# Attention with mirrored squares: consecutive key tiles, V in one transfer, and logits turned on VectorE

## The chip, the cores and the metric

The kernel runs on one core of a Trainium2 chip. A core has a matrix engine (TensorE, PE in the profile; PEld is its loading of weights), a vector engine (VectorE, DVE), a scalar engine (ScalarE, ACT), a general one (GpSimd, POOL), and a queue that issues transfers (SyncE, SP). Each of them takes its instructions in order; between them semaphores decide. Data lie in SBUF, 128 partitions wide, and matmul results in PSUM. The metric is the device time of one execution in microseconds.

## The reference

Eight batches of 2496 tokens go through an attention without softmax, and its output through a mixture of experts of which each token uses one.

```python
def _attn_ref(u, v, z):
    scale = 1.0 / S
    scores = scale * np.matmul(z, z.transpose(0, 2, 1))
    attn = np.maximum(scores, 0.0) ** 2
    out = np.matmul(attn, v)
    return u * out

def _moe_ref(x, w_gate, w1, w2):
    logits = x @ w_gate
    expert_idx = np.argmax(logits, axis=1)
    ...
    for e in range(E):
        xe = x[mask]
        h = np.maximum(xe @ w1[e], 0.0)
        out[mask] = gate_w[mask, None] * (h @ w2[e])
```

Here S is 2496, the width of `u` and `v` 256, that of `z` 64, and there are 8 experts with 1024 hidden values. Queries and keys are the same `z`, so the matrix of scores is symmetric: the square for query i and key j is that for query j and key i.

## The kernel before

**Numbers.** Matmuls take fp32r operands, which hold fewer bits than fp32. Each operand is therefore split into a rounded part and a remainder (`hi` and `lo` for the squares, two halves of `vt` for V), and products of the parts are summed. The sum over keys of one pair of key tiles is 12 matmuls (L319, L321, L322).

**Loops.** A batch has five chunks of queries, four of 512 and one of 448, and 20 key tiles of 128, taken in ten pairs `kp`. The last 64 rows of the last tile repeat tokens and count only with a remainder's part. A step is one (batch, chunk, pair); 400 steps are written out in one list, and step s computes the scores of step s + 2 (`LA = 2`) before its own weighted sums. The compiler's scheduler orders what the list leaves open. Work given to `pinned` stays behind what was last issued on each engine.

**Scores.** `scores` (L272) computes a pair's scores in PSUM, relu (L295) and square (L296) on ACT, `hi` on ACT or DVE (L298), `lo` on DVE (L300). By symmetry this is done only for pairs in key chunk `cc >= c`. Where `cc > c`, `turn` (L241) transposes the squares in blocks of 32 x 32 on DVE (L255), and writes 1 MB for four key tiles to DRAM (L258, `scr`). `bring` (L260) reads it back with partitions and blocks exchanged (L266), into a slot `s`, up to eight steps before it is used. For `cc < c`, `scores` then only splits what was brought (L285 on ACT, L286 on DVE).

**Key tiles.** A key tile isn't made of consecutive tokens. In the first four key chunks, tile i of a chunk holds tokens i, i + 4, i + 8 and so on (`rows_of`, L232); in the last, three tiles hold every third of 384 tokens and the fourth the 128 behind them. With this order, the turned squares lie in runs of 128 consecutive queries when they are read.

**V.** V must be in the order of the key tiles. `fetch_v` (L127) issues four transfers of 32 partitions for a pair in the first four key chunks, and six and four smaller ones for the two pairs of the last, all on SP, into two buffers `vr`. `split_v` (L143) makes the two parts: a cast on ACT (L146), a subtraction on POOL (L148). V of the next batch is fetched one pair a step during the last chunk of a batch, and split one step later, since it takes the place of the pair that was just used; in batch 0 it is fetched two steps ahead.

**From the sums to the experts.** Behind a chunk's ten steps `gate_x` (L336) multiplies by `u`, splits the result, and puts work into the list `bg`, of which one item is pinned to each step from the third of the next chunk on: `logits` (L365), `turn_rows` (L353), two empty items, `choose` (L407), `exps`, `place` (L428). `logits` multiplies by 16 columns of weights (8 experts, 2 parts), which leaves 16 partitions by n tokens in PSUM. ACT copies them (L374), DVE separates the 16-bit halves of each value (L379, L380), and two DMA transposes on SP (L382) put tokens on partitions. `choose` joins the halves (two copies, L411) and finds the expert; `place` computes each token's row in its expert's list, writes the rows (L453 on SP) and scatters token numbers (L458 on POOL). `turn_rows` transposes the rows themselves with four more DMA transposes (L363).

Behind all steps the experts run over tiles of tokens (`tiles`, `up` L735, `down` L756 and L758), with rows gathered on POOL and turned on SP (L703).

Of the kernel before, what the change touches and what calls it, by code (L numbers as in the profile page):

```python
# [23 lines left out]
E = 8  # L24
# [24 lines left out]
def fused_kernel(ctx: ExitStack, tc: tile.TileContext, zt, ut, v, wg, wcat, out):  # L49
# [77 lines left out]
    def fetch_v(b, kp):  # L127

        vr = vraw[b, kp] = sb.tile([P, 2, D], F32, name="vr", bufs=2)
        c, h = divmod(kp, 2)  # L130
        if c < NC_ - 1:
            for g in range(G):
                src = v[b, :, G * c + g, :].rearrange("(k i) d -> k i d", i=G)
                nc.sync.dma_start(vr[g * R:(g + 1) * R], src[:, 2 * h:2 * h + 2])
            return
        for i in range(2 * h, min(2 * h + 2, 3)):
            for k in range(3):
                lo, hi = -(-(k * P - i) // 3), min(P, -(-((k + 1) * P - i) // 3))
                nc.sync.dma_start(vr[lo:hi, i - 2 * h], v[b, bass.ds(3 * lo + i - k * P, hi - lo, step=3), G * c + k, :])  # L139
        if h:  # L140
            nc.sync.dma_start(vr[:, 1, :], v[b, :, NK - 1, :])
# [31 lines left out]
    wg2 = const.tile([P, 2, 2, E], FR, name="wg2")  # L173
# [33 lines left out]
    def constants():  # L207
        nc.vector.tensor_copy(wg2[:, :, 0, :], wg_sb)
        nc.vector.tensor_tensor(wg2[:, :, 1, :], wg_sb, wg2[:, :, 0, :].bitcast(F32), op=ALU.subtract)
# [31 lines left out]
    def turn(b, c, cc, h, a):  # L241
# [6 lines left out]
        t4_ = tt.rearrange("p (s r e) -> p s r e", s=G, r=4)  # L248
        for i in range(2):
            k = 2 * h + i  # L250
            if cc < NC_ - 1:
                to = t4_[:, :, :, k::4]
            else:
                to = t4_[:, :, :, k:3 * R:3] if k < 3 else t4_[:, :, :, 3 * R:]
            nc.vector.transpose(out=to, in_=a[:, i].rearrange("p (s q r) -> p s r q", s=G, r=4))  # L255
# [4 lines left out]
    def bring(b, cc, c):  # L260
# [7 lines left out]
        brought[b, cc, c] = st.rearrange("p (g r e) -> p r g e", g=G, r=4)  # L268
# [3 lines left out]
    def scores(b, c, kp):  # L272
# [63 lines left out]
    def gate_x(b, c, acc):  # L336
# [28 lines left out]
        def logits():  # L365
# [10 lines left out]
            if n < QC:  # L376
                nc.vector.memset(lp[:, :, n:QC], 0)
# [581 lines left out]
```

## Time and profile before

| | us |
|---|---|
| median of three runs | 2562.58 (2561.98 to 2563.81) |
| the profiled execution | 2576.18 |
| its span, first to last instruction | 2574.3 |
| PE busy | 2333.1 |
| DVE busy | 1754.4 |
| ACT busy | 1446.9 |
| POOL busy | 735.3 |
| mean granted TensorE clock | 0.948 |

The profile is of one execution, 0.5% above the median of the others. Lines such as L255 are those of the kernel listed above. Attention fills the first 1640 us or so, the experts the rest. A group of instructions is shown with its count, busy time in us, mean ns of one, and, behind the second bar, the idle time of its engine just before, with what ended it. A window gives for each engine its busy time and number of instructions. The granted clock is a share of full speed. SPq is the queue of SP, whose entries show how long it took to issue a transfer, not how long the transfer took.

### The profile page before, as it was taken

Reading aid. Unit: us, or ns where it says so; the run is one execution under the profiler, and the core shown is the slowest. Engines: PE = TensorE matmul, PEld = TensorE weight load, DVE = VectorE, ACT = ScalarE, POOL = GpSimd, SP = SyncE. Lnnn points to the kernel's source line nnn. Section 1 sums busy time; section 2 is a strip of 40 time slices with the busy share of each in tenths; the row PEclk is TensorE's granted clock in tenths of the full one; section 3 lists DMA queues with packets and bytes.
Section 4 is the critical chain, followed back from the end, with each engine's and each line's share of the span. In section 5 each row is a group of like instructions: output and inputs, shape, how many; then the busy total and the mean of one; then the engine's idle time right before and its main releaser. Section 6 shows DMA issues by size and latency. Waiting matters only on the chain.

```text
span 2574.3 us, 32216 instructions
## 1 busy us (share of the span) xinstructions
PE 2333.1 (91%) x10872; PEld 1947.0 (76%) x10872; DVE 1754.4 (68%) x3027; ACT 1446.9 (56%) x1993; POOL 735.3 (29%) x707
## 2 busy tenths in 40 slices
PE   7997987898889799789899798799999999999998
PEld 5785776687668677667678677688888888888887
DVE  6877866787777787766786786475556566556554
ACT  4755754664655575555565574345456456556554
POOL 2112113013112112112212221454445445445431
PEclk8998998999889899899899899899999999999999
DMA  5695896986878877688779589775456456547540
GB/s 161 172 185 118 216 160 105 194 176 124 191 153 152 193 165 149 177 162 153 166 170 171 129 198 201 134 177 143 129 148 171 144 153 174 150 151 188 143 138 26
DMA packets 329693, 406.00 MB, mean 158 GB/s; under 512 B 201708, under 2 KB 245498, under 8 KB 310064
## 3 DMA queue, kind: packets, MB, share of 16 engines
q1 hardware_dynamic: 298128, 284.77, 51.8%
q0 software_dynamic: 31392, 119.10, 15.9%
q8 instruction: 87, 1.43, 0.2%
q14 instruction: 86, 0.70, 0.1%
HBM read 233.67 MB, written 127.32 MB: 140 GB/s over the span
## 4 chain that ended last, share of the span: by engine, by line
PE 54%; DMA 17%; DVE 16%; issue 4%; SPq 4%; ACT 4%; POOL 1%; DVEq 0%; ACTq 0%; POOLq 0%
PE ph L735 16%; PE y L756 11%; DMA vr<-in_v_dram 7%; DMA lg<-lp 7%; PE acc L322 6%; PE acc L321 6%; PE y L758 6%; PE acc L319 6%; DVE s L255 5%; DVE tlo L300 3%; SPq L139 2%; DVE tlo L286 2%; PE ps_s L293 2%; PE ps_s L294 1%; ACT tf L295 1%
## 5 line engine op out<-in xcount | busy, mean ns | idle before, releaser
L321 PE MATMUL acc<-tlo,t 128*128 128x512 f32 (+1 forms) x1520 | 616.5, 406 | 85.0 <-DVE tlo L300 53.9
L319 PE MATMUL acc<-thi,t 128*128 128x512 f32 (+1 forms) x1600 | 603.5, 402 | 54.5 <-ACT thi L285 26.5
L322 PE MATMUL acc<-thi,t 128*128 128x512 f32 (+1 forms) x1600 | 638.3, 400 | 3.7 <-POOL t L148 3.2
L321 PEld LDWEIGHTS acc<-tlo,t 128*128 128x128 f32 x1520 | 299.2, 197 | 162.1 <-DVE tlo L300 70.9
L319 PEld LDWEIGHTS acc<-thi,t 128*128 128x128 f32 x1600 | 312.6, 197 | 120.7 <-ACT thi L285 29.6
L740 DVE SCALAR_TENSOR_TENSOR t<-ph,t 128x512 fp32r<-128x512 f32 (+1 forms) x328 | 220.8, 675 | 267.4 <-ACT t L739 265.2
L756 PE MATMUL y<-t,t 128*128 128x512 f32 x1062 | 382.3, 400 | 8.4 <-DVE tf L768 8.4
L739 ACT ACTIVATE t<-ph 128x512 fp32r<-128x512 f32 (+1 forms) x328 | 193.7, 591 | 331.1 <-PE ph L735 280.9
L735 PE MATMUL ph<-thi,t 128*128 128x512 f32 (+2 forms) x1248 | 372.0, 362 | 2.9 <-ACT thi L717 2.7
L322 PEld LDWEIGHTS acc<-thi,t 128*128 128x128 f32 x1600 | 314.4, 197 | 63.8 <-POOL t L148 4.9
L255 DVE STREAM_TRANSPOSE s<-tf 128x512 f32<-128x512 f32 x320 | 340.3, 1117 | 32.7 <-ACT tf L296 32.4
L295 ACT ACTIVATE tf<-ps_s 128x1024 f32<-128x1024 f32 (+1 forms) x240 | 241.2, 1013 | 181.8 <-DVE tlo L300 67.1
L458 POOL DMA_INDIRECT lst<-toks,posi x160 | 189.3, 1183 | 519.3 <-DVE posi L450 462.3
L286 DVE TENSOR_TENSOR tlo<-s,thi 128x768 fp32r<-128x768 f32 (+1 forms) x224 | 213.7, 978 | 120.1 <-ACT thi L285 119.3
L758 PE MATMUL y<-t,t 128*128 128x256 f32 x1062 | 288.6, 283 | 0.0
L300 DVE TENSOR_TENSOR tlo<-tf,thi 128x1024 fp32r<-128x1024 f32 (+1 forms) x200 | 244.8, 1232 | 28.4 <-ACT thi L298 27.3
L735 PEld LDWEIGHTS ph<-thi,t 128*128 128x128 f32 x1248 | 224.7, 189 | 40.4 <-ACT thi L717 3.7
L296 ACT ACTIVATE tf<-tf 128x1024 f32<-128x1024 f32 (+1 forms) x240 | 250.0, 1052 | 3.7
L756 PEld LDWEIGHTS y<-t,t 128*128 128x128 f32 x1062 | 199.4, 191 | 49.7 <-issue 8.7
L285 ACT CAST thi<-s 128x768 fp32r<-128x768 f32 (+1 forms) x224 | 166.2, 770 | 125.9 <-PE acc L322 111.4
L735 PE MATMUL ph<-tlo,t 128*128 128x512 f32 (+2 forms) x624 | 225.1, 361 | 4.3 <-DVE tlo L718 4.3
L758 PEld LDWEIGHTS y<-t,t 128*128 128x128 f32 x1062 | 203.1, 191 | 11.1
(230 smaller groups left out, 3430.0 us busy)
## 6 DMA issues: line engine op xcount, KB each, us to landing
scr<-s SPq DMA_DIRECT2D x80, 1024.0 KB
s<-scr SPq DMA_DIRECT2D x320, 256.0 KB
xrows<-rows SPq DMA_DIRECT2D x32, 544.0 KB
vr<-in_v_dram SPq DMA_DIRECT2D x256, 64.0 KB
u<-in_ut_dram SPq DMA_DIRECT2D x32, 512.0 KB
zr<-in_zt_dram SPq DMA_DIRECT2D x40, 256.0 KB
u<-in_ut_dram SPq DMA_DIRECT2D x8, 448.0 KB
xrows<-rows SPq DMA_DIRECT2D x8, 408.0 KB
```

What stands on the lines that cost most here:

```text
L255: nc.vector.transpose(out=to, in_=a[:, i].rearrange("p (s q r) -> p s r q", s=G, r=4))
L286: nc.vector.tensor_tensor(l, a, h.bitcast(F32), op=ALU.subtract)
L295: nc.scalar.activation(a[:, :, :n], ps[:, :, :n], AF.Relu)
L296: nc.scalar.activation(a[:, :, :n], a[:, :, :n], AF.Square)
L300: nc.vector.tensor_tensor(lo[:, :, :n], a[:, :, :n], hi[:, :, :n].bitcast(F32), op=ALU.subtract)
L319: nc.tensor.matmul(acc[d][:, :n], lhsT=vh, rhs=hi[:, i, :n], start=first and i == 0, stop=False)
L321: nc.tensor.matmul(acc[d][:, :n], lhsT=vh, rhs=lo[:, i, :n], start=False, stop=False)
L322: nc.tensor.matmul(acc[d][:, :n], lhsT=vl, rhs=hi[:, i, :n], start=False, stop=last and i == 1)
L735: nc.tensor.matmul(o, lhsT=w1[:, part, dd, fs], rhs=xx[:, dd, :n], start=p == 0, stop=p == 5)
L740: nc.vector.scalar_tensor_tensor(hl[:, :m], ph[:, :m], 0.0, hh[:, :m].bitcast(F32), op0=ALU.max, op1=ALU.subtract)
L756: nc.tensor.matmul(y, lhsT=hh[:, cs], rhs=w2[:, f % 2].rearrange("p i d -> p (i d)"), start=f == 0, stop=False)
L758: nc.tensor.matmul(y[:, 0:D], lhsT=hl[:, cs], rhs=w2[:, f % 2, 0, :], start=False, stop=f == NF - 1)
```

## The change

Key tiles become 128 consecutive tokens. V is then loaded as it lies: one transfer of a whole pair. The matmul's key operand is a contiguous slice of `z`. `turn` does both tiles of a pair in one DVE transpose that reads contiguously and writes runs of 32; the slot's layout becomes (block, tile, group, 32). `scores` reads the brought squares in runs of 32 and puts them in order on writing, in one operation for each chunk, the last included. The logits' weights are padded with zeros from 16 to 32 columns, and four DVE transposes of 32 partitions read the logits out of PSUM straight into `lw`, so that ACT's copy, the separation of halves, the two DMA transposes and the two joining copies go, as does the buffer `lt` that shared its place with `zr`. For the short chunk, POOL clears the part of `lw` that isn't written.

```diff
     def fetch_v(b, kp):
-        vr = vraw[b, kp] = sb.tile([P, 2, D], F32, name="vr", bufs=2)
-        c, h = divmod(kp, 2)
-        if c < NC_ - 1:
-            for g in range(G):
-                src = v[b, :, G * c + g, :].rearrange("(k i) d -> k i d", i=G)
-                nc.sync.dma_start(vr[g * R:(g + 1) * R], src[:, 2 * h:2 * h + 2])
-            return
-        for i in range(2 * h, min(2 * h + 2, 3)):
-            for k in range(3):
-                lo, hi = -(-(k * P - i) // 3), min(P, -(-((k + 1) * P - i) // 3))
-                nc.sync.dma_start(vr[lo:hi, i - 2 * h], v[b, bass.ds(3 * lo + i - k * P, hi - lo, step=3), G * c + k, :])
-        if h:
-            nc.sync.dma_start(vr[:, 1, :], v[b, :, NK - 1, :])
+        vraw[b, kp] = sb.tile([P, 2, D], F32, name="vr", bufs=2)
+        nc.sync.dma_start(vraw[b, kp], v[b, :, 2 * kp:2 * kp + 2, :])
...
-    wg2 = const.tile([P, 2, 2, E], FR, name="wg2")
+    wg2 = const.tile([P, 2, R], FR, name="wg2")
...
+        nc.vector.memset(wg2.bitcast(F32), 0.0)
...
     def turn(b, c, cc, h, a):
...
-        t4_ = tt.rearrange("p (s r e) -> p s r e", s=G, r=4)
-        for i in range(2):
-            k = 2 * h + i
-            if cc < NC_ - 1:
-                to = t4_[:, :, :, k::4]
-            else:
-                to = t4_[:, :, :, k:3 * R:3] if k < 3 else t4_[:, :, :, 3 * R:]
-            nc.vector.transpose(out=to, in_=a[:, i].rearrange("p (s q r) -> p s r q", s=G, r=4))
+        to = tt.rearrange("p (s t i k) -> p i t s k", s=G, t=4, i=4)[:, 2 * h:2 * h + 2]
+        nc.vector.transpose(out=to, in_=a.rearrange("p i (t s k) -> p i t s k", t=4, s=G))
...
     def scores(b, c, kp):
...
-            st = brought[b, cc, c][:, kp % 2 * 2:kp % 2 * 2 + 2]
-            if c < NC_ - 1:
-                runs = [(st, slice(0, QC), G)]
-            else:
-                runs = [(st[:, :, :, 0:3 * R], slice(0, 3 * P), G), (st[:, :, 0:2, 3 * R:], slice(3 * P, n), 2)]
-            for a, to, g in runs:
-                h, l = [x[:, :, to].rearrange("p j (g e) -> p j g e", g=g) for x in (hi, lo)]
-                nc.scalar.copy(h, a)
-                nc.vector.tensor_tensor(l, a, h.bitcast(F32), op=ALU.subtract)
+            a = brought[b, cc, c][:, kp % 2 * 2:kp % 2 * 2 + 2].rearrange("p j i g k -> p (j i) g k")
+            h, l = [x.rearrange("p j (i g k) -> p (j i) g k", i=4, g=G) for x in (hi, lo)]
+            nc.scalar.copy(h, a)
+            nc.vector.tensor_tensor(l, a, h.bitcast(F32), op=ALU.subtract)
...
-            hl_k = rows_of(ztiles[b, cc][0], cc, kp % 2 * 2 + i)
+            hl_k = ztiles[b, cc][0][:, (kp % 2 * 2 + i) * P:(kp % 2 * 2 + i + 1) * P]
...
     def gate_x(b, c, acc):
...
-        lg = sb.tile([P, 2, QC // P, 2 * E], U16, name="lg")
+        lw = sb.tile([P, QC // P, R], F32, name="lw", bufs=2)
+        if n < QC:
+            nc.gpsimd.memset(lw[n % P:P, ns - 1], 0.0)
...
-            lt = sb.tile([P, QC], F32, name="lt", tag="zr", bufs=2)[0:2 * E]
-            nc.scalar.copy(lt[:, :n], pt[0:2 * E, :n])
-            lp = sb.tile([P, 2, QC], U16, name="lp", tag="lp")[0:2 * E]
...
-            nc.vector.tensor_copy(lp[:, 0, :n], src[:, 1, :])
-            nc.vector.tensor_copy(lp[:, 1, :n], src[:, 0, :])
-            for h in range(2):
-                nc.sync.dma_start_transpose(out=lg[:, h], in_=lp[:, h, :])
+            for g in range(G):
+                w = -(-(n - g * R) // P)
+                src = pt[0:R].rearrange("p (s g k) -> p g s k", g=G, k=R)[:, g, 0:w]
+                nc.vector.transpose(out=lw[g * R:(g + 1) * R, 0:w], in_=src)
...
         def choose():
-            lw = sb.tile([P, QC // P, 2 * E], F32, name="lw", bufs=2)
-            lwh = lw.bitcast(U16).rearrange("p s (e h) -> p s e h", h=2)
-            for h in range(2):
-                nc.vector.tensor_copy(lwh[:, :, :, 1 - h], lg[:, h])
```

More of the change, by code (lines that the diff above doesn't have):

```diff
@@ L207, in constants @@
     def constants():
-        nc.vector.tensor_copy(wg2[:, :, 0, :], wg_sb)
-        nc.vector.tensor_tensor(wg2[:, :, 1, :], wg_sb, wg2[:, :, 0, :].bitcast(F32), op=ALU.subtract)
+        nc.vector.memset(wg2.bitcast(F32), 0.0)
+        nc.vector.tensor_copy(wg2[:, :, 0:E], wg_sb)
+        nc.vector.tensor_tensor(wg2[:, :, E:2 * E], wg_sb, wg2[:, :, 0:E].bitcast(F32), op=ALU.subtract)
         for ti, tf in iotas:
@@ L267, in bring @@
                               d.rearrange("(g q) (s e) -> s q g e", g=G, s=G)[q])
-        brought[b, cc, c] = st.rearrange("p (g r e) -> p r g e", g=G, r=4)
+        brought[b, cc, c] = st.rearrange("p (g t i k) -> p t i g k", g=G, t=4, i=4)
     free = list(range(NSLOT))
@@ L369, in logits @@
                 for xx in (xh, xl):
-                    nc.tensor.matmul(pt[0:2 * E, :n], lhsT=wg2[:, i].rearrange("p a e -> p (a e)"), rhs=xx[:, i, :n],
-                                     start=m == 0, stop=m == 3)
+                    nc.tensor.matmul(pt[0:R, :n], lhsT=wg2[:, i], rhs=xx[:, i, :n], start=m == 0, stop=m == 3)
                     m += 1
-            lt = sb.tile([P, QC], F32, name="lt", tag="zr", bufs=2)[0:2 * E]
-            nc.scalar.copy(lt[:, :n], pt[0:2 * E, :n])
-            lp = sb.tile([P, 2, QC], U16, name="lp", tag="lp")[0:2 * E]
-            if n < QC:
-                nc.vector.memset(lp[:, :, n:QC], 0)
-            src = lt[:, :n].bitcast(U16).rearrange("p (n h) -> p h n", h=2)
-            nc.vector.tensor_copy(lp[:, 0, :n], src[:, 1, :])
-            nc.vector.tensor_copy(lp[:, 1, :n], src[:, 0, :])
-            for h in range(2):
-                nc.sync.dma_start_transpose(out=lg[:, h], in_=lp[:, h, :])
+            for g in range(G):
+                w = -(-(n - g * R) // P)
+                src = pt[0:R].rearrange("p (s g k) -> p g s k", g=G, k=R)[:, g, 0:w]
+                nc.vector.transpose(out=lw[g * R:(g + 1) * R, 0:w], in_=src)
         bg.append(logits)
         bg.append(turn_rows)
-        bg.extend([nothing] * 2 + route(b * S + q0, n, ns, lg, xr))
+        bg.extend([nothing] * 2 + route(b * S + q0, n, ns, lw, xr))
     def nothing():
@@ L392, in fused_kernel, with route @@
     lst1 = lst.rearrange("a b -> (a b)").unsqueeze(1)
-    def route(t0, n, ns, lg, xr):
+    def route(t0, n, ns, lw, xr):
         mlast = n - (ns - 1) * P
```

4 lines of the change are left out of this document (removed).

## The prediction

> **What bounds the kernel now.** First the page: the chain of work that ended last, by engine and by line.
>
> ```profile
> PE 54%; DMA 17%; DVE 16%; issue 4%; SPq 4%; ACT 4%; POOL 1%; DVEq 0%; ACTq 0%; POOLq 0%
> PE ph L735 16%; PE y L756 11%; DMA vr<-in_v_dram 7%; DMA lg<-lp 7%; PE acc L322 6%; PE acc L321 6%; PE y L758 6%; PE acc L319 6%; DVE s L255 5%; DVE tlo L300 3%; SPq L139 2%; DVE tlo L286 2%; PE ps_s L293 2%; PE ps_s L294 1%; ACT tf L295 1%
> ```
>
> The chain runs through PE, but 16% of it is two kinds of transfer, V (`vr`) and the turned logits (`lg`), and both are edited. Then the windows: the first period up to the stall behind its batch, six whole periods of one batch, the last period, the experts. Columns: length, PE, PEld, DVE, ACT, POOL busy, granted clock, DMA share, GB/s.
>
> ```profile
> 0.00:242.40 242.40, 207.09 (x846) 165.58 (x846) 176.80 (x266) 137.94 (x165) 56.31 (x67) 0.93 0.68 159
> 242.40:1460.60 1218.20, 1061.26 (x4531) 872.33 (x4531) 895.59 (x1459) 710.97 (x841) 233.21 (x217) 0.93 0.77 163
> 1460.60:1642.50 181.90, 157.12 (x667) 127.66 (x667) 128.49 (x257) 106.17 (x128) 42.40 (x39) 0.93 0.92 194
> 1642.50:2574.30 931.80, 907.68 (x4829) 781.39 (x4829) 553.52 (x1048) 491.78 (x861) 403.43 (x386) 0.99 0.52 143
> ```
>
> A batch takes 1218.2/6 = 203.0 us, of which PE is idle 26.2. DVE (149 us a batch) and ACT (118) have room, so attention isn't bound by an engine's throughput but by waits. The experts (931.8 us, PE 97% busy) use nothing edited; I leave them as they are. What PE waits for, and what those engines waited for in turn (total us, times, longest):
>
> ```profile
> PE ps_s L293 <- ACT tf L295: 69.8, 9, 12.4
> PE acc L321 <- DVE tlo L300: 53.9, 35, 7.2
> PE acc L321 <- DVE tlo L286: 30.7, 13, 7.4
> PE acc L319 <- ACT thi L285: 26.5, 8, 6.4
> ...
> ACT t L146 <- DMA vr<-in_v_dram: 207.7, 25, 19.2
> ...
> DVE lw L411 <- DMA lg<-lp: 123.7, 27, 11.0
> ...
> DVE lp L379 <- ACT lt L374: 86.4, 8, 14.1
> ```
>
> ACT takes its instructions in order: while L146 waits for V, no relu (L295) or cast (L285) behind it starts, and PE runs dry. DVE does the same at L411 for `lg`. One batch in the timeline of PE (start, duration, idle before it and releaser), with the last such gap of the stage:
>
> ```profile
> 298.91 0.80 PE L321 MATMUL acc<-tlo,t 128*128 128x512 f32 x1 [3.14 <-DVE tlo L300]
> 340.45 0.80 PE L321 MATMUL acc<-tlo,t 128*128 128x512 f32 x1 [7.45 <-DVE tlo L286]
> 406.87 1.11 PE L319 MATMUL acc<-thi,t 128*128 128x448 f32 x2 [6.38 <-ACT thi L285]
> 448.19 0.81 PE L293 MATMUL ps_s<-t,t 128*128 128x512 f32 x1 [8.22 <-ACT tf L295]
> 1636.61 1.11 PE L319 MATMUL acc<-thi,t 128*128 128x448 f32 x2 [9.20 <-DVE thi L298]
> ```
>
> The first two and the last lie behind `lg`, the third and fourth behind V; the chain puts the transfers just ahead of them (start, duration):
>
> ```profile
> 3.14 3.36 DMA zr<-in_zt_dram
> ...
> 380.67 0.23 PE acc L322
> 395.06 9.80 DMA vr<-in_v_dram
> 410.43 0.37 PE acc L322
> 416.56 0.21 PE acc L322
> 438.16 14.70 DMA vr<-in_v_dram
> 495.51 13.71 DMA lg<-lp
> ```
>
> A gap also costs afterwards. The matmul of 448 columns takes 0.37 us at 410 and 0.21 at 416, as the clock shows:
>
> ```profile
> 408.00:410.00 2.00, 1.06 (x3) 0.98 (x4) 1.94 (x4) 1.10 (x3) 0.74 (x1) 0.50 0.38 75
> ...
> 916.00:917.00 1.00, 0.90 (x4) 0.78 (x5) 1.00 (x3) 0.97 (x2) 0.00 (x0) 1.00 0.00 0
> ```
>
> At 408, behind the 6.38 us gap, the clock is 0.50; at 916, behind a gap of little over 1 us, it stays at 1.00. So long gaps are dearer than they look.
>
> **What a batch would take without waits.** The code issues 118 matmuls a chunk for the sums, 4 for its logits, and 40, 32, 24, 16 and 8 for the scores of the five chunks: 600 of 512 columns and 130 of 448. At 0.228 and 0.206 us each (the 0.23 and 0.21 above) they take 136.8 + 26.8, with about 1.4 for the places: 165 us. The loss is 203.0 - 165 = 38 us a batch: 26.2 idle and 11.8 at half clock.
>
> **The change part by part.**
>
> *Logits.* It removes the two transposing DMAs, the ACT copy and the four DVE copies of a chunk, and adds four DVE transposes of 32x128 out of PSUM, 40 chunks in all.
>
> ```profile
> L382 SPq DMA_TRANSPOSE lg<-lp x80: 1125/1162/3697, 93.4 to 1656.8; - x80
> ...
> L374 ACT COPY lt<-pt 16x512 f32<-16x512 f32 x32 | 18.3, 571 | 0.0
> L411 DVE COPY lw<-lg 128x64 uint16<-128x64 uint16 x80 | 14.5, 204 | 125.3 <-DMA lg<-lp 123.7
> L380 DVE COPY lp<-lt 16x512 uint16<-16x512 uint16 x32 | 13.2, 414 | 0.0
> ```
>
> DVE work: away 2 x 0.41 + 2 x 0.20 = 1.23 us; added four ops, none of which the trace has. The bounds are 0.20 us (L411) and 0.41 (L380) each; I take 0.25, near L411 for its 128 columns of 16 bits, so 1.0. No difference on an engine with room. ACT loses 0.57 a chunk, SP 2.3. What counts is the wait: thirteen gaps from 298.91 to 1636.61 sit behind it, 66.6 us; eight of them, 44.9 us, in the six periods. A period has 2 V gaps and 8/6 of these, 3.3 slow stretches in all, so one costs 11.8/3.3 = 3.5 us. **Saved: 44.9/6 + 8/6 x 3.5 = 12 us a batch.** The added wait is DVE's for the four matmuls L370: behind it stand `lo` and the turned squares, for which PE waits. Today's DVE waits at the same place through ACT (L379, mostly under 1 us, 8 long ones when V holds ACT), so I price it at 0.
>
> *V.* One transfer of 128 partitions, two rows of 1 KB to a partition, replaces four of 32 partitions, or six and four in the last key chunk, for each pair: 336 issues become 80, the same bytes.
>
> ```profile
> L134 SPq DMA_DIRECT2D vr<-in_v_dram x256: 311/425/1646, 1.3 to 1433.9; - x128
> L146 ACT CAST t<-vr x80: 602/617/626, 5.1 to 1458.6; 128x512 fp32r<-128x512 f32 x80
> L148 POOL TENSOR_TENSOR t<-vr,t x78: 1255/1298/2399, 22.8 to 1459.3; 128x512 fp32r<-128x512 f32 x78
> ...
> 427.39 9.05 SPq L139 DMA_DIRECT2D vr<-in_v_dram  x9
> ```
>
> (Three durations are least, median and most, in ns.) During its last chunk a batch fetches the next one's ten V pairs into two buffers, so a pair is issued when POOL is done with the pair but one before. A pair then costs issue + landing + 0.6 (ACT) + 1.3 (POOL), halved for two buffers; PE's step there is 12 x 0.206 = 2.5 us, and scores run two steps, 5 us, ahead. The landing of such a transfer isn't in the trace. Lower bound: `zr`, also 128 partitions of 2 KB, 3.36 us into an empty queue; a pair every (0.4 + 3.4 + 1.9)/2 = 2.9 us falls 4 us behind over ten steps, which the 5 us cover: no gap. Upper bound: 9.80, as today at the start of the chunk, where the squares being brought back (1 MB) and `u` (0.46 MB) stand ahead in the queue and don't change; that makes 6 us a pair, and the gaps stay. I take 5 us, nearer to `zr` for its shape: 3.7 us a pair, 12 behind, 7 beyond the cover, of which I put 6 as PE's idle time, with one slow stretch. Today the V gaps are 69.8 + 26.5 and some 8 us of gaps that follow on, over seven boundaries: 15 us, with two slow stretches. **Saved: 15 + 7 - 6 - 3.5 = 12.5 us a batch.** The worst transfers are those of pairs 8 and 9, where SP issues nine pieces in 9.05 us and the last lands 14.70 us later.
>
> These pieces have 42 or 43 partitions. The Trainium skill, "DMA: Bandwidth & Descriptors", section "Why a DMA increments its semaphore by 16 and not by 1", says that a transfer uses the largest number of engines up to 16 that divides its outermost sizes: one engine for 43, sixteen for 128. The 14.70 against 9.80 us agrees, though no row shows the engines. By that rule the gap at pairs 8 and 9 goes whole (rival 2).
>
> *Turned squares.* One DVE transpose of 1024 contiguous elements replaces two of 512 that read and write every fourth, 160 times.
>
> ```profile
> L255 DVE STREAM_TRANSPOSE s<-tf 128x512 f32<-128x512 f32 x320 | 340.3, 1117 | 32.7 <-ACT tf L296 32.4
> L300 DVE TENSOR_TENSOR tlo<-tf,thi 128x1024 fp32r<-128x1024 f32 x192 | 236.1, 1238 | 28.3 <-ACT thi L298 27.3
> L286 DVE TENSOR_TENSOR tlo<-s,thi 128x1024 fp32r<-128x1024 f32 x96 | 117.0, 1222 | 26.3 <-ACT thi L285 25.6
> L286 DVE TENSOR_TENSOR tlo<-s,thi 128x768 fp32r<-128x768 f32 x64 | 69.5, 1085 | 93.8 <-ACT thi L285 93.7
> L286 DVE TENSOR_TENSOR tlo<-s,thi 128x128 fp32r<-128x128 f32 x64 | 32.3, 505 | 0.0
> ```
>
> L300 passes 1024 contiguous elements in 1.24 us, L255 takes 2 x 1.12. These bound the new one; I take 1.24, since the stride of four is what sets L255 apart. Saved: 160 x 1.0 us of DVE, 20 a batch. Little of it is on the path: only in the first chunk does DVE come near PE (1.24 + 2.24 us a step, with the casts, the gating and the splits, against 16 x 0.228 = 3.65), and the short gaps left over in a period, 26.2 - 15 - 7.5 = 3.7 us, are in part its doing. **Saved: 1 us a batch.**
>
> *Squares read in runs of 32.* ACT's cast and DVE's subtraction take 160 x 1024 elements; in the last chunk one op replaces two (1085 + 505 ns by 1222, 64 times, 23 us of DVE off the path). That runs of 32 cost more than runs of 128 is not in the trace: between nothing and the twofold of L255, about 5 us a batch where the chunk's DVE would fill up. I take nothing: a run of 32 is still contiguous.
>
> *Kept out of the sum.* Key tiles of consecutive tokens and weights of 32 columns instead of 16 leave the matmuls' count and moving columns alone; the memset of `wg2` stands once, at the start.
>
> **The sum.** A period: 12 + 12.5 + 1 = 25.5, times six 153. First batch: its V gaps are those of one boundary and several smaller ones at the start, no long `lg` gap: 12.5 + 9 = 22. Last period: 66.6 - 44.9 = 22 us of `lg` gaps with three slow stretches, no V; but rows of the experts' first tiles queue there too (DMA share 0.92), so I take 18 of 32. Together 193 of the profiled execution, whose span is 2574.3 and whose own time 2576.2; the median of the runs is 2562.6, and I take the saving off that: **2370 us**.
>
> **The rivals.**
>
> 1. *V stays late* (18%). For it: landings of 9.80 us at a place where queue order and bytes stay. Against: SP's issue and the small pieces go. V's 12.5 is lost seven times: 2370 + 88 = 2458.
> 2. *The gap at pairs 8 and 9 goes whole* (10%), and only that at the chunk's start stays. For it: 14.70 us there against 9.80 for whole pieces. Half of the 6 idle and the slow stretch go, 6.5 us seven times: 2325.
> 3. *Nearly all waits go* (8%). Landing by `zr`, no slow stretches: 33 of 38 us a batch, six times, 38 of the first and 30 of the last, 266: 2297. The Trainium skill, "TensorE: Matmul & The Clock Gate", Part 1, points this way: the clock halves only after an idle window of some 3.4 us. By that rule gaps of 3 us would cost no slow stretch, 3.5 us seven times less than my sum. The rows at 408 and 916 agree.
> 4. *Strided access isn't what costs* (4%): the transposes stay at 2.2 us a pair, or the reads slow down; the first chunk stays full on DVE, 5 us a batch: 2410.
> 5. *DVE now hangs on PE* (4%). The transposes wait for L370; `lo` stands behind them, PE waits for `lo`. Against: L379 waits for the same matmuls today, through ACT's copy, without such gaps. If each of the 40 chunks had a gap as at 340 (7.45 + 3.5 = 11 us), 440 less the 193: 2810, slower. It decides from 193/40 = 5 us a chunk.
> 6. *No effect* (2%): transfers bound attention as it is (share 0.77), other transfers take over the waits: 2563.
>
> **How the numbers follow.** The forecast has 54%. The range 2290 to 2470 holds it, rivals 1 to 4 and the bounds of landing, transpose and reads; outside are 5 and 6 and the tails of all. Faster by over 0.2% (5 us, about what a measurement can tell from no change): all but 5 and 6, with 1 in 100 off for mishaps, 0.93; slower 0.05; same 0.02.
>
> **What would show it.** No wait at L411 and no gap of PE behind `lg`; L146's wait for V (207.7) down to under 100; transposes of 1024 at about 1.24 us; a period near 177 us at a granted clock of 0.97 or more; the experts unchanged at about 930. Wrong would be the forecast if ACT still waits 10 us and more for V at each boundary, or if DVE waits for L370 for over 5 us a chunk.

## The result, and the profile after

| | before | after |
|---|---|---|
| median of four runs | 2563.19 us (2561.98 to 2563.99) | 2372.62 us (2369.95 to 2373.46) |
| the profiled execution | 2576.18 us | 2372.18 us |
| its span | 2574.3 us | 2370.4 us |
| mean granted TensorE clock | 0.948 | 0.982 |

The ratio is 0.9255 (95% interval 0.9239 to 0.9271); 2370 was forecast. First the chain of work that ended last in the changed kernel, by engine and by line.

```profile
PE 77%; DVE 9%; DMA 5%; issue 4%; ACT 3%; POOL 2%; SPq 0%; ACTq 0%; POOLq 0%; DVEq 0%
```

PE's share of the chain went from 54% to 77%, that of transfers from 17% to 5%. The line of the chain by lines no longer has `lg`, and V stands there with 3% instead of 7%. Now the windows of the changed kernel, cut at the first logits matmul of the short chunk, which comes once a batch: the start, six whole periods, the last period, the experts.

```profile
0.00:211.65 211.65, 191.00 (x811) 149.27 (x812) 153.52 (x227) 133.96 (x151) 52.37 (x65) 0.97 0.74 177
211.65:1273.15 1061.50, 1012.36 (x4531) 826.33 (x4530) 814.14 (x1286) 694.60 (x763) 240.49 (x222) 0.98 0.88 186
1273.15:1442.44 169.29, 155.73 (x704) 126.13 (x702) 123.76 (x239) 105.46 (x118) 44.68 (x42) 0.98 1.01 199
1442.44:2370.40 927.96, 903.92 (x4829) 778.63 (x4829) 552.91 (x1048) 490.85 (x860) 409.33 (x388) 0.99 0.52 147
```

The same cut through the six periods of the kernel before:

```profile
222.88:1441.31 1218.43, 1061.12 (x4532) 872.29 (x4531) 895.40 (x1458) 710.91 (x840) 234.24 (x217) 0.93 0.77 163
```

A period fell from 1218.43/6 = 203.1 us to 1061.50/6 = 176.9. PE's idle time in it fell from (1218.43 - 1061.12)/6 = 26.2 to (1061.50 - 1012.36)/6 = 8.2 us. The rest of the gain, 8.1 us, is in PE's busy time, for the same number of matmuls: the clock went from 0.93 to 0.98. The experts took 931.8 us before and 928.0 after. What PE waits for now, with the waits of ACT and DVE that were named before (total us, times, longest):

```profile
ACT t L134 <- DMA vr<-in_v_dram: 103.8, 29, 9.1
PE acc L293 <- DVE tlo L272: 30.1, 15, 3.3
...
DVE lw L349 <- PE pt L344: 20.2, 16, 2.3
...
PE acc L291 <- ACT thi L257: 19.3, 7, 4.4
```

The 69.8 us at the scores behind `tf` and the 123.7 of DVE for `lg` are gone. What is left of V is 19.3 us in seven gaps (L291 behind ACT's cast). PE's largest wait is now for DVE's `tlo` (L272), 15 times, up to 3.3 us. One boundary in PE's timeline shows them all:

```profile
363.23 1.12 PE L291 MATMUL acc<-thi,t 128*128 128x448 f32 x2 [4.40 <-ACT thi L257]
...
381.07 0.50 PE L293 MATMUL acc<-tlo,t 128*128 128x512 f32 x1 [1.34 <-DVE tlo L272]
...
394.37 0.79 PE L293 MATMUL acc<-tlo,t 128*128 128x512 f32 x1 [3.28 <-DVE tlo L272]
```

The first is the start of the short chunk, where PE waits behind a late transfer of V. The other two lie in the next batch's first chunk; at their place, behind pairs 8 and 9, the kernel before had its 8 to 12 us gaps. The priced operations, from the groups and from the views of their tiles (least, median, most in ns, where three are given):

```profile
L349 DVE STREAM_TRANSPOSE lw<-pt x160: 274/306/311, 81.3 to 1455.1; 32x128 f32<-32x128 f32 x144, 32x96 f32<-32x96 f32 x16
L232 DVE STREAM_TRANSPOSE s<-tf x160: 1175/1237/1247, 13.4 to 1371.6; 128x1024 f32<-128x1024 f32 x160
...
L257 ACT CAST thi<-s x160: 1027/1048/1057, 65.8 to 1423.5; 128x1024 fp32r<-128x1024 f32 x160
L258 DVE TENSOR_TENSOR tlo<-s,thi x160: 1181/1224/1995, 67.2 to 1424.9; 128x1024 fp32r<-128x1024 f32 x160
```

A transpose of 1024 contiguous elements takes 1.24 us, as priced. Reading in runs of 32 costs nothing: L258 takes 1224 ns where the same subtraction took 1222 with runs of 128.

### The profile page after: what moved, and what is told of

It reads as the page before. It is cut to its first block, busy times and chain, and to the rows that moved or that the text cites. A ratio compares the mean times of both kernels' runs of the same rounds, so it can differ in the third digit from the quotient of the medians.

```text
span 2370.4 us, 31257 instructions
## 1 busy us (share of the span) xinstructions
PE 2263.0 (95%) x10872; PEld 1880.4 (79%) x10872; DVE 1644.3 (69%) x2796; ACT 1424.9 (60%) x1889; POOL 746.9 (32%) x715
## 4 chain that ended last, share of the span: by engine, by line
PE 77%; DVE 9%; DMA 5%; issue 4%; ACT 3%; POOL 2%; SPq 0%; ACTq 0%; POOLq 0%; DVEq 0%
PE ph L698 17%; PE y L719 12%; PE acc L294 11%; PE acc L291 11%; PE acc L293 11%; PE y L721 6%; PE ps_s L265 4%; PE ps_s L266 4%; DMA vr<-in_v_dram 3%; DVE tlo L272 2%; PE pt L344 1%; DVE t L123 1%; DMA s<-scr 1%; DVE tlo L258 1%; POOL t L136 1%
## 5 line engine op out<-in xcount | busy, mean ns | idle before, releaser
L293 PE MATMUL acc<-tlo,t 128*128 128x512 f32 (+1 forms) x1520 | 598.4, 394 | 40.6 <-DVE tlo L272 30.1
L294 PE MATMUL acc<-thi,t 128*128 128x512 f32 (+1 forms) x1600 | 626.5, 393 | 4.5 <-POOL t L136 4.4
L291 PE MATMUL acc<-thi,t 128*128 128x512 f32 (+1 forms) x1600 | 588.8, 393 | 27.2 <-ACT thi L257 19.3
L291 PEld LDWEIGHTS acc<-thi,t 128*128 128x128 f32 x1600 | 305.9, 192 | 91.0 <-ACT thi L257 22.7
L293 PEld LDWEIGHTS acc<-tlo,t 128*128 128x128 f32 x1520 | 290.4, 191 | 106.9 <-DVE tlo L272 37.2
L294 PEld LDWEIGHTS acc<-thi,t 128*128 128x128 f32 x1600 | 306.3, 192 | 62.3 <-POOL t L136 6.8
L421 POOL DMA_INDIRECT lst<-toks,posi x160 | 186.9, 1168 | 414.9 <-DVE posi L413 303.0
L258 DVE TENSOR_TENSOR tlo<-s,thi 128x1024 fp32r<-128x1024 f32 x160 | 200.2, 1251 | 141.9 <-ACT thi L257 138.6
L272 DVE TENSOR_TENSOR tlo<-tf,thi 128x1024 fp32r<-128x1024 f32 (+1 forms) x200 | 248.0, 1246 | 50.1 <-ACT thi L270 48.0
L232 DVE STREAM_TRANSPOSE s<-tf 128x1024 f32<-128x1024 f32 x160 | 197.0, 1235 | 81.8 <-ACT tf L268 77.9
L257 ACT CAST thi<-s 128x1024 fp32r<-128x1024 f32 x160 | 167.5, 1047 | 116.2 <-PE acc L294 103.8
L719 PEld LDWEIGHTS y<-t,t 128*128 128x128 f32 x1062 | 198.0, 189 | 49.2 <-issue 8.7
L270 ACT CAST thi<-tf 128x1024 fp32r<-128x1024 f32 (+1 forms) x176 | 182.8, 1039 | 67.6 <-PE acc L294 56.2
```

Source lines behind the costliest of these rows:

```text
L232: nc.vector.transpose(out=to, in_=a.rearrange("p i (t s k) -> p i t s k", t=4, s=G))
L258: nc.vector.tensor_tensor(l, a, h.bitcast(F32), op=ALU.subtract)
L272: nc.vector.tensor_tensor(lo[:, :, :n], a[:, :, :n], hi[:, :, :n].bitcast(F32), op=ALU.subtract)
L291: nc.tensor.matmul(acc[d][:, :n], lhsT=vh, rhs=hi[:, i, :n], start=first and i == 0, stop=False)
L293: nc.tensor.matmul(acc[d][:, :n], lhsT=vh, rhs=lo[:, i, :n], start=False, stop=False)
L294: nc.tensor.matmul(acc[d][:, :n], lhsT=vl, rhs=hi[:, i, :n], start=False, stop=last and i == 1)
```

## The experiments

Each run is described by its ratio to the kernel before on the same chip, by its period (the mean of six distances between the logits matmuls of the short chunk, as above), and by the start of the experts' first matmul, which ends attention. The later runs were on other chips, where the kernel before took 2579 to 2617 us and the experts, with the same code, up to 952: so ratios of different groups are not set against each other, and the period is the main reading. "Chip" marks runs with a common kernel before (c and e are one chip at two times).

| run | chip | median us | ratio (95%) | period | attention ends |
|---|---|---|---|---|---|
| before | a | 2563.19 | | 203.1 | 1642.5 |
| changed kernel | a | 2372.62 | 0.9255 (0.9239 to 0.9271) | 176.9 | 1442.4 |
| logits by DMA again | b | 2430.03 | 0.9444 (0.9399 to 0.9488) | 184.2 | 1493.1 |
| V in four pieces of 32 | b | 2389.58 | 0.9281 (0.9242 to 0.9320) | 176.2 | 1437.1 |
| pairs 8, 9 in pieces of 43 and 42 | b | 2457.61 | 0.9537 (0.9497 to 0.9576) | 185.0 | 1522.0 |
| before with only the new logits | b | 2492.78 | 0.9665 (0.9626 to 0.9704) | 192.1 | 1560.7 |
| changed kernel again | c | 2394.35 | 0.9272 (0.9245 to 0.9298) | 177.3 | 1445.1 |
| V's subtraction on DVE | c | 2381.36 | 0.9212 (0.9184 to 0.9239) | 173.7 | 1431.1 |
| V a step earlier | c | 2374.02 | 0.9185 (0.9156 to 0.9213) | 173.9 | 1429.1 |
| both | c | 2373.26 | 0.9183 (0.9154 to 0.9212) | 173.4 | 1432.1 |
| every transpose twice | d | 2474.11 | 0.9485 (0.9452 to 0.9519) | 186.1 | 1522.3 |
| four V buffers, three pairs ahead | d | 2350.12 | 0.8993 (0.8968 to 0.9017) | 170.0 | 1410.3 |
| the same, subtraction on DVE | d | 2328.52 | 0.8931 (0.8907 to 0.8956) | 166.8 | 1378.2 |
| strided transposes | e | 2421.98 | 0.9261 (0.9239 to 0.9283) | 178.5 | 1461.3 |

### Logits alone, and everything but the logits

The changed kernel with ACT's copy, the separation of halves and the two DMA transposes back:

```diff
-            for g in range(G):
...
-                nc.vector.transpose(out=lw[g * R:(g + 1) * R, 0:w], in_=src)
+            nc.scalar.copy(lt[:, :n], pt[0:2 * E, :n])
+            nc.vector.tensor_copy(lp[:, 0, :n], src[:, 1, :])
+            nc.vector.tensor_copy(lp[:, 1, :n], src[:, 0, :])
+            for h in range(2):
+                nc.sync.dma_start_transpose(out=lg[:, h], in_=lp[:, h, :])
```

> The changed kernel with the logits turned by two DMA transposes again, as before. Theory (the logits' wait holds DVE, 12 us a batch): about 90 us slower than the changed kernel, 2445 to 2475, DVE waiting over 80 us in all for the transfer lg. Rival (that wait was long mostly because V's many small transfers stood in the same queue, so it shrinks without them): at most 40 us slower, under 2415, DVE waiting under 50 us for lg.

And the opposite: the kernel before, with only the logits turned on DVE, V and the key tiles as they were.

> The kernel before with only the logits' part of the change (VectorE out of PSUM). Theory: 70 to 110 us faster than the kernel before, 2455 to 2495, with V's gaps at the batch boundaries as before (ACT waiting some 200 us for V). Rival (both waits overlap at the boundary, so one alone brings little): under 50 us faster, over 2513.

The waits in the first of them:

```profile
DVE lw L382 <- DMA lg<-lp: 142.0, 40, 11.1
ACT t L134 <- DMA vr<-in_v_dram: 99.4, 29, 14.0
PE acc L291 <- ACT thi L257: 48.6, 7, 9.9
PE acc L293 <- DVE tlo L258: 28.9, 10, 6.3
```

The waits in the second:

```profile
ACT t L146 <- DMA vr<-in_v_dram: 191.0, 26, 14.5
PE ps_s L294 <- ACT tf L296: 69.3, 9, 12.0
PE acc L320 <- ACT thi L286: 35.4, 9, 9.3
```

Alone, the new logits take 203.1 - 192.1 = 11.0 us off a period and 82 us off attention; V's gap behind `tf` stays nearly as it was (69.3 against 69.8). On top of the rest they are worth less, 184.2 - 176.9 = 7.3 us a period and 51 us of attention. DVE waits even longer for `lg` than before (142.0 against 123.7), but PE has seven gaps of 4.0 to 6.3 us behind it where it had thirteen, up to 9.2. At the same time V's gap at the start of the short chunk grows from 19.3 to 48.6 us. So the two parts aren't independent. The first run's time lies between its theory and its rival, its wait for `lg` (over 80 us) came as the theory had it; the second came as its theory had it.

### How V is cut

```diff
-        nc.sync.dma_start(vraw[b, kp], v[b, :, 2 * kp:2 * kp + 2, :])
+        for g in range(G):
+            nc.sync.dma_start(vraw[b, kp][g * R:(g + 1) * R], v[b, g * R:(g + 1) * R, 2 * kp:2 * kp + 2, :])
```

> The changed kernel with each V pair fetched in four transfers of 32 partitions instead of one. Theory (what cost was the odd pieces of 42 and 43 partitions, and the queue ahead at the start of the last chunk): 0 to 25 us slower than the changed kernel, 2372 to 2398. Rival (the number of issues on SP cost): 50 us or more slower, over 2422, with gaps of 8 us and more behind V at each boundary.

```diff
+        if kp < NKP - 2:
+            nc.sync.dma_start(vraw[b, kp], v[b, :, 2 * kp:2 * kp + 2, :])
+            return
+        for i in range(2):
+            if kp == NKP - 1 and i == 1:
+                nc.sync.dma_start(vraw[b, kp][:, 1, :], v[b, :, NK - 1, :])
+                continue
+            for lo, hi in ((0, 43), (43, 86), (86, P)):
+                nc.sync.dma_start(vraw[b, kp][lo:hi, i], v[b, lo:hi, 2 * kp + i, :])
```

> The changed kernel with pairs 8 and 9 of V fetched in pieces of 43, 43 and 42 partitions (six and four transfers), as many as before but of consecutive tokens. Theory (odd pieces land late and hold ACT): the gap of some 10 us in the first chunk of each batch comes back, 60 to 100 us slower than the changed kernel, 2432 to 2472. Rival (the strided rows of 1 KB, not the pieces' sizes, made them late): under 25 us slower, under 2398.

Four pieces of 32 partitions for every pair, as many issues as before in eight of ten pairs, leave the period where it was, 176.2 against 176.9 us, as the theory had it. Two things offset each other in it: V's gap at the start of the short chunk grows from 2.6 to 5.1 us a period, and the gap of 3.3 us in the first chunk is gone. Ten pieces for pairs 8 and 9 alone, most of 43 or 42 partitions, bring the gap behind them back, in every batch:

```profile
PE acc L299 <- ACT thi L278: 40.1, 8, 6.9
```

```profile
408.25 1.22 PE L299 MATMUL acc<-thi,t 128*128 128x512 f32 x2 [5.65 <-ACT thi L278]
...
414.04 0.80 PE L301 MATMUL acc<-tlo,t 128*128 128x512 f32 x1 [2.80 <-DVE tlo L280]
```

The period is 185.0, 8.1 us longer, as the theory had it. Of that, 5.6 us are idle time (13.7 against 8.2): these gaps came, and the one of 3.3 us at 394 in the changed kernel isn't there. The other 2.5 are PE's busy time at a lower clock (0.954 against 0.979). So it isn't the number of transfers, nor their bytes (64 KB in a piece of 32 partitions, 43 KB in one of 43). Nor is it the rows, which are 1 KB here instead of 2: the pieces of 32 partitions in the kernel before had rows of 1 KB too, and those issued from 419.43 to 423.78 landed in 1.8 to 2.4 us. What is left is the number of partitions.

The Trainium skill, "DMA: Bandwidth & Descriptors", section "Why a DMA increments its semaphore by 16 and not by 1", says that a transfer uses the largest number of engines up to 16 that divides the slowest dimension of both sides: one for 43, fourteen for 42, sixteen for 32 or 128. The trace agrees. But for one early count, a piece of 43 partitions reports its landing in one part, one of 42 in fourteen, one of 32 or 128 in sixteen. And of a whole piece issued behind such pieces, at 399.29, 15 parts have landed after 2.03 us and the sixteenth only after 6.24:

```profile
399.29 6.24 DMA vr<-in_v_dram
```

### The transposes of the squares

First each transpose was done twice:

```diff
         nc.vector.transpose(out=to, in_=a.rearrange("p i (t s k) -> p i t s k", t=4, s=G))
+        nc.vector.transpose(out=to, in_=a.rearrange("p i (t s k) -> p i t s k", t=4, s=G))
```

> The changed kernel with each transpose of 1024 elements done twice, the second time with the same result: 160 x 1.235 us = 198 us of work back on VectorE, about what the two strided ones of 1117 ns had taken beyond one of 1235 ns (160 x 1.0 = 160 us), at the same place and without a transfer. Theory (VectorE has room, the halved transposes were worth 1 us a batch): the span grows by 5 to 40 us, the first chunk's steps get gaps behind tlo of a microsecond or two. Rival (the transposes were a large part of the gain, since V's relus and the sums of the first chunk queue behind them): the span grows by 80 us or more, at most the 198 us of the work.

The period came out at 186.1, 9.2 us longer, which looks like the rival. But the extra time isn't where DVE works. POOL at one boundary, first in the changed kernel, then in this run, and PE in this run:

```profile
346.99 0.96 POOL L421 DMA_INDIRECT lst<-toks,posi  x1 [0.30 <-PE acc L294]
347.94 0.17 POOL L322 MEMSET rows<- 128x64 int32 x1
348.56 4.03 POOL L136 TENSOR_TENSOR t<-vr,t 128x512 fp32r<-128x512 f32 x2 [0.45 <-ACT t L134]
```

```profile
364.29 0.15 POOL L323 MEMSET rows<- 128x64 int32 x1 [14.25 <-DMA xrows<-rows]
...
369.60 0.96 POOL L422 DMA_INDIRECT lst<-toks,posi  x1 [0.30 <-issue]
370.58 2.48 POOL L136 TENSOR_TENSOR t<-vr,t 128x512 fp32r<-128x512 f32 x2
```

```profile
387.51 1.12 PE L292 MATMUL acc<-thi,t 128*128 128x448 f32 x2 [19.23 <-ACT thi L258]
```

The compiler's scheduler, presumably because it had other durations to plan with, put the clearing of the next buffer of rows (L323) ahead of a chunk's scatters instead of behind them. The clearing waits 14.25 us until the buffer has been written out, and the scatters and V's first two subtractions stand behind it. These subtractions free V's buffers; so V's next pairs were issued at 371.88, where the changed kernel issued them at 350.39, and PE stood for 19.23 us. The run measures that order and not the transposes; it settles nothing about them. So the old pair of strided transposes was put into the changed kernel, where POOL's order at this place stays as in the changed kernel (the next expectation, written before that closer look, speaks of scatters that had moved; it was the clearing):

```diff
-        nc.vector.transpose(out=to, in_=a.rearrange("p i (t s k) -> p i t s k", t=4, s=G))
+        t4_ = tt.rearrange("p (s r e) -> p s r e", s=G, r=4)
+        for i in range(2):
+            to = t4_[:, :, :, 2 * h + i::4]
+            nc.vector.transpose(out=to, in_=a[:, i].rearrange("p (s q r) -> p s r q", s=G, r=4))
```

> The changed kernel with the two strided transposes of the kernel before in place of each one of 1024 elements: the squares are turned in a wrong order, so the output differs and the experts get other tokens, and only the attention stage is read. In the run with every transpose done twice, GpSimd's scatters had moved ahead of V's subtraction at the end of the fourth chunk, and V's third pair was issued 20 us later; here that order is as in the changed kernel. Theory (VectorE has room, the halved transposes were worth about 1 us a batch): the period is 177 to 180 us, against 176.85, and VectorE's extra 1 us a kept pair shows as short gaps in the first chunk only. Rival (the first chunk, which keeps 16 transposes in steps of 3.65 us, fills up on VectorE, and V's casts behind it come late): a period of 184 us or more, 7 us a batch or more for the transposes.

```profile
L234 DVE STREAM_TRANSPOSE s<-tf 128x512 f32<-128x512 f32 x320 | 340.3, 1125 | 26.7 <-ACT tf L270 26.2
```

The strided form costs its 2 x 1.125 us again, and the period is 178.5: 1.6 us more than on chip a, 1.3 more than in the repeated run. That lies in the theory's range, and the rival's 184 didn't come. But it is a net of several things: the gap of 3.3 us in the first chunk is gone here too, short gaps behind `tlo` stand there instead, and V's gap is 4.5 us a period against 2.6 and 3.6. What the transposes cost by themselves isn't measured cleanly. Attention ends 16 to 19 us later; beyond the seven periods some of this lies at V's gaps (7.31 us at 369 against 4.40 at 363) and in the last batch, and its cause is open.

### What is left: V's landing and a collision on DVE

The changed kernel was run again for the next three:

> The changed kernel once more, on the chip of the three runs beside it, as their measure. Both theories: its ratio to the kernel before as measured already, 0.9255 within 0.004.

Its ratio came out at 0.9272, as expected.

DVE and POOL just ahead of the gap at 394.37, in the changed kernel:

```profile
389.19 1.23 DVE L232 STREAM_TRANSPOSE s<-tf 128x1024 f32<-128x1024 f32 x1
390.34 2.83 DVE L123 TENSOR_TENSOR t<-zr,t 64x512 fp32r<-64x512 f32 x1
393.10 1.21 DVE L272 TENSOR_TENSOR tlo<-tf,thi 128x1024 fp32r<-128x1024 f32 x1
```

```profile
390.11 2.51 POOL L136 TENSOR_TENSOR t<-vr,t 128x512 fp32r<-128x512 f32 x2
```

A subtraction of 512 elements takes DVE 2.83 us while POOL makes two of V's subtractions; L272 stands behind it, and PE waits 3.28 us. Taking V's subtraction from POOL:

```diff
-        eng = nc.gpsimd if b or kp > 1 else nc.vector
+        eng = nc.vector
```

> The changed kernel with every subtraction of the V split on VectorE instead of GpSimd (0.69 us each there, 78 of them). Theory (the new gap of 3.3 us in each first chunk comes from a VectorE subtraction of the z split that takes 2.8 instead of 0.7 us while GpSimd does its own on V): the z subtraction L123 back to 0.7 us in the mean, that gap gone, 15 to 35 us faster than the changed kernel. Rival (VectorE is simply full in the first chunk): no faster, or up to 15 us slower.

The same line in the groups, first in the changed kernel, then in this run:

```profile
L123 DVE TENSOR_TENSOR t<-zr,t 64x512 fp32r<-64x512 f32 x40 | 39.9, 997 | 1.5 <-POOL t L119 1.0
```

```profile
L123 DVE TENSOR_TENSOR t<-zr,t 64x512 fp32r<-64x512 f32 x40 | 26.8, 670 | 0.4
```

The mean falls from 997 to 670 ns, the gap of 3.3 us is gone, and the period is 3.6 us shorter than in the repeated run, although DVE has 78 operations more. Between the medians it is 13 us, just under the 15 to 35 of the theory. In the last batch gaps of 5.20 and 11.11 us appeared behind squares still on their way, which took part of it back.

The second is the gap at the start of the short chunk. The chain of waits, the queue of SP and ACT show it for one boundary of the changed kernel:

```profile
350.39 10.25 DMA vr<-in_v_dram
```

```profile
341.77 1.75 SPq L243 DMA_DIRECT2D s<-scr  x4
343.62 0.57 SPq L142 DMA_DIRECT2D u<-in_ut_dram  x1
...
350.39 2.58 SPq L129 DMA_DIRECT2D vr<-in_v_dram  x2
...
367.52 1.00 SPq L129 DMA_DIRECT2D vr<-in_v_dram  x2
```

```profile
370.24 0.62 ACT L134 CAST t<-vr 128x512 fp32r<-128x512 f32 x1 [4.75 <-DMA vr<-in_v_dram]
```

The first of these is the next batch's third pair; its first two had taken the buffers over 130 us earlier. It lands 10.25 us after its issue, while one issued at 367.52 has landed by 370.24, 2.7 us later. The squares (1 MB) and `u` (0.5 MB) were issued just ahead of it, but it doesn't wait for them: by the completions in the trace they had landed by 349.27 and 350.33. Still under way were POOL's scatters of token numbers (L421), and over the landing of V the DMA engines moved 51 GB/s (the last column), where they had moved 203 before:

```profile
344.06 1.36 POOL L421 DMA_INDIRECT lst<-toks,posi  x1 [0.30 <-issue]
```

```profile
344.00:350.39 6.39, 6.39 (x33) 5.84 (x33) 3.87 (x4) 3.32 (x5) 5.27 (x6) 1.00 0.91 203
350.39:360.64 10.25, 8.44 (x41) 7.00 (x39) 4.10 (x7) 1.05 (x1) 2.32 (x2) 1.00 0.65 51
```

The scatters issued at 344.06, 345.72 and 346.99 land at 359.20, 360.21 and 360.47, V's pair at 360.64. At all seven boundaries this pair lands 0.2 to 1.7 us behind the last scatter. The run with every transpose twice tells the two causes apart, since there V was issued long behind `u`:

```profile
356.28 0.57 SPq L142 DMA_DIRECT2D u<-in_ut_dram  x1
371.88 1.57 SPq L129 DMA_DIRECT2D vr<-in_v_dram  x2
```

`u` had landed by 369.52 and nothing else of SP's was under way, and yet the pair took 13.05 us; it landed 0.16 us behind the last scatter. At that run's first boundary (188.47), with squares and `u` still ahead and the last scatter through within 0.6 us, it took 4.07 us. In the changed kernel, pairs with no scatter under way land in 2.5 to 4.0 us, and in 4.2 to 6.1 with squares ahead of them. So the queue ahead costs something, but V's late pair is late beside POOL's scatters. Why scatters, which move few bytes, and V finish together isn't shown, and no run moved the scatters: that would be the next experiment. The runs that follow were planned on the other reading, that the queue ahead of V makes it late. Fetching V one step earlier, with two buffers as before:

```diff
-            fetch_v(b + 1, order_of(b + 1, 0)[j])
...
+            if j + 1 < NKP:
+                fetch_v(b + 1, order_of(b + 1, 0)[j + 1])
+        if c == NC_ - 2 and j == 6 and b + 1 < B:
+            fetch_v(b + 1, order_of(b + 1, 0)[0])
```

> The changed kernel with each V pair of the next batch fetched one step earlier, the first one in the fourth chunk, ahead of the last squares brought back and of u. Theory (the gap at the start of the last chunk is the first V pair standing behind these in the queue): that gap of 2 to 4 us goes, 15 to 40 us faster than the changed kernel. Rival (two buffers limit the rate, so the wait moves to a later pair): within 8 us of the changed kernel, a gap behind V at a later step.

> Both of the two edits before. Theory: their gains add, 30 to 70 us faster than the changed kernel, near 2320. Rival: no more than the better of the two alone, since they wait for the same thing.

The gap stayed at 3 to 5 us. The late pair is the third, as it was before: it has to wait for a buffer, which POOL's subtraction frees, and an earlier step doesn't change that. It landed 10.7 us after its issue. The run is 20 us faster than the repeated one all the same, as much as the theory had, but not by that gap: of the 3.3 us that the period fell, 2.4 are idle time, much of it in the first chunk, where the gap of 3.3 us became two of about 1. Both edits together gave no more than either (173.4, and 21 us), as their rival had it, and their last batch had a gap of 19.52 us behind the squares. So both buffers and time were given:

```diff
-        vraw[b, kp] = sb.tile([P, 2, D], F32, name="vr", bufs=2)
+        vraw[b, kp] = sb.tile([P, 2, D], F32, name="vr", bufs=4)
...
-            fetch_v(b + 1, order_of(b + 1, 0)[j])
...
+            if j + 3 < NKP:
+                fetch_v(b + 1, order_of(b + 1, 0)[j + 3])
+        if c == NC_ - 2 and 4 <= j < 7 and b + 1 < B:
+            fetch_v(b + 1, order_of(b + 1, 0)[j - 4])
```

> The changed kernel with four buffers for V instead of two, and the first three pairs of the next batch fetched during the fourth chunk, each later pair three steps ahead; GpSimd keeps the subtraction. Theory (the gap of 3.2 us at the start of the last chunk, and the one that moved to the third pair when V was only fetched a step earlier, come from two buffers and landings of 7 to 11 us): the gap goes, seven times 3 to 5 us with its slow stretch, 20 to 35 us off the changed kernel, a ratio of 0.912 to 0.918 to the kernel before. Rival (the transfers of the last period are what bounds it, and V's pieces moved earlier only push the squares and rows back): within 10 us of the changed kernel, with new gaps behind the squares brought back or behind the rows.

> The same with V's subtraction all on VectorE as well. Theory (the subtraction of z took 2.83 us beside GpSimd's subtraction of V, and its first-chunk gap of 3.3 us goes with it): both gaps gone, a period near 170 us against 177, 35 to 50 us off the changed kernel, a ratio of 0.906 to 0.913. Rival (as in the run where V was fetched a step earlier and subtracted on VectorE: the last batch's chunk is bound by transfers, and gaps of 10 to 20 us there take the gain back): a ratio of 0.916 to 0.922.

With four buffers V's gap goes at most boundaries (170.0 us a period). DVE's slow subtraction goes with it, though POOL keeps its own (L123 takes 697 ns in the mean), so the gain isn't V's gap alone. The ratios lie below those expected, which were set by earlier chips; the kernel before took 2610 us on this one. With the subtraction on DVE as well the six periods are these:

```profile
207.35:1208.35 1001.00, 991.67 (x4532) 813.27 (x4531) 798.69 (x1346) 696.16 (x763) 152.57 (x162) 1.00 0.99 196
```

PE is busy 991.67/6 = 165.3 us of 166.8, at a clock of 1.00: the 165 us of a batch without waits, to within half a microsecond. This is the fastest kernel of all runs: 2328.5 us in five runs (2326.9 to 2337.7) against 2372.6 of the changed kernel, on a chip where the kernel before was slower (2610). The changed kernel itself wasn't run on that chip, so the step from it is best read from the period, 10.1 us, and from the end of attention, 64 us earlier. What is left is in the last batch: its period is 177.7 us, with a gap of 5.04 us behind the squares and one of 11.25 ahead of the experts, and DMA's busy share in the six periods is 0.99.

## Why the prediction was right

Waits were what bounded the kernel, and the mechanism for the logits held with its size. The mechanism for V didn't come as it was put: rival 2's came, which saves more. Gaps that stood in no term took about as much back, so that the sum came out, which is in part luck.

**What bounded the kernel.** Waits, not throughput: shown. A period lost 26.2 us of idle time and 11.8 at half clock; of these 18.0 and 8.1 went, where the terms of the forecast add up to 17.5 (7.5 at `lg`, 9 at V, 1) and 8.2 (4.7 and 3.5). The 165 us that a batch takes without waits are PE's busy time in the best run. One reading was loose: the lines of the chain put V and `lg` at 7% each, 14 together and not 16.

**Logits.** Forecast 12 us a batch; alone 11.0, on top of the other edits 7.3. The mechanism is right: no wait for `lg` is left. A transpose out of PSUM takes 0.306 us and not 0.25, so four take 1.22 where 1.23 went, and DVE's work didn't change. DVE's new wait for the matmuls is 20.2 us in 16 times, at most 2.3, with no gap of PE from it: pricing it at nothing held, and rival 5, the slower case, didn't come.

**V.** Forecast 12.5, with the squares 13.5; measured with the squares 184.2 against 203.1, or 176.9 against 192.1: 18.9 or 15.2 us a period. The sum took a landing of 5 us for every pair, so that pairs would fall behind one after another, and its upper bound had the squares and `u` ahead in the queue as the reason for a long landing. The traces show something else. Most pairs land in 2.5 to 4.0 us; one late pair a boundary, the third, takes 6.4 to 10.3 and finishes with POOL's scatters, which stood in no term. PE loses 2.3 to 4.4 us by it at six boundaries of seven, where 6 us were left in, and the gap at pairs 8 and 9 goes whole. That was rival 2's mechanism, at 10%, for the reason it gave, and the pieces of 43 partitions brought the gap back.

**What took it back.** The gaps of 3.3 and 1.4 us in the first chunk, 4.7 a period, stood in no term. V's subtractions on POOL, no longer held up at pairs 8 and 9, now run beside DVE's subtraction of `z`: the gap of 3.3 went with them to DVE, while one of 1.5 stayed in that chunk, and its cause is open. With V's 19.3/7 = 2.8 us they make 7.5 us of idle time where 6 were forecast for V, and so the sum came out: 26.2 us a period against 25.5. Nothing in the prediction makes these 4.7 us replace what V no longer cost: that is luck.

**Turned squares.** 1.24 us a transpose, as taken. The strided form made the period 1.3 to 1.6 us longer, a net of several gaps, where 1 was forecast. Runs of 32 cost nothing, as taken; rival 4 is out.

**First batch, last period, medians.** Cut as the prediction cut them (behind the 846th and the 5376th matmul), the first stretch fell from 242.4 to 221.2 us, 21 where 22 were forecast; the six periods from 1218.1 to 1065.3, 153 as forecast; the last one from 182.0 to 156.0, 26 and not 18. The experts saved 4 where nothing was forecast. So the span lost 204, not 193. The profiled execution of before was 13 us above its median, that of after at its median; so 191 was measured between the medians. That the forecast of 193 off the median came so close is luck again: its sum was 11 us short of what the span lost, and the medians differ by 13 us less than the profiled executions.

**What was to show it.** No wait for `lg`, the transposes, the period, the clock of 0.98 and the experts came as said. ACT's wait for V, 103.8 us, stayed just above the 100 that was set. And one sign against the forecast came: ACT waits for V over 10 us at each boundary, 12.3 to 16.1 us in all (9.11 + 4.75 + 1.20 + 0.99 at the one shown), though no single wait is longer than 9.1. The time was right all the same, because only 2.8 us a boundary of it reach PE. The sign was set on the wrong engine.

## What to carry to other kernels

Price a transfer by what else is under way: the same 256 KB landed in under 4 us, or in 6 to 13 beside another engine's scatters, and a mean of the two describes neither. See from the completions what a transfer really finishes with; what stands ahead of it in its queue may have landed long ago. Where a gap is removed, look at what the freed engine will now run beside, and give a prefetch buffers as well as an earlier issue: the earlier issue alone did nothing for a pair that waits for a buffer. When a run is to isolate a cost, look first whether the scheduler kept the order of the other engines.

## What the hardware showed beyond that

DVE's subtraction of 64x512 takes 0.67 us by itself and 2.83 us when it starts beside two subtractions of POOL (390.34 and 390.11 above). It ends at 393.17, 0.55 us behind POOL's second one (392.62), and POOL's own take their usual 1.3 us each. The same 2.83 us come at this place in six batches, so it seems to have stood still rather than run slowly. The Trainium skill, "SBUF — State Buffer", section "Who interferes with whom", says that a DVE instruction with two inputs in SBUF contends with a GpSimd instruction that reads SBUF, and that such contention is an exclusive lock. The traces agree, and here DVE was shut out over both of POOL's instructions, not only over the first.

A gap's cost in clock isn't given by its length. The two microseconds behind the gap of 1.34 us at 381, behind that of 3.28 at 394, and the four behind one of 3.29 at the same place of a later batch:

```profile
381.10:383.10 2.00, 2.00 (x9) 1.66 (x10) 2.00 (x4) 1.01 (x3) 0.15 (x1) 1.00 0.50 169
394.40:396.40 2.00, 2.00 (x5) 1.61 (x6) 1.97 (x3) 2.00 (x3) 0.00 (x0) 0.50 1.39 264
...
750.60:752.60 2.00, 2.00 (x7) 1.63 (x8) 1.97 (x3) 2.00 (x3) 0.00 (x0) 0.82 0.65 187
752.60:754.60 2.00, 2.00 (x6) 1.57 (x5) 1.93 (x5) 2.00 (x3) 0.00 (x0) 0.50 1.22 237
```

The clock is 1.00 behind the first and 0.50 behind the second; behind the third it falls to 0.50 only after a while. Summed over the 8 us behind it, the second gap costs 3.0 us of full clock, the third 1.7. In the changed kernel, gaps of 2.59 to 4.40 us cost 1.7 to 3.2 us each, and those of 1.34 to 1.50 nothing; one of 1.85 us (546.87) cost 1.7 and one of 1.88 (900.20) nothing. In the repeated run two of six gaps of 3.3 us (749.55 and 1282.25) cost nothing, the other four 1.7. So the 3.5 us that the prediction put on each long gap is more than any of these gaps cost, and rival 3's condition, that gaps of 3 us cost no slow stretch, holds for some of them only.
